# Operands of the first four blocks copied across the partition halves by ScalarE, and a planner that counts on late softmax loads

## The chip, the cores and the metric

The kernel runs on one core of one Trainium2 chip. The metric is the device time of one execution in microseconds (us); the time before is the median of three runs. One further execution was taken with the hardware profiler, and all rows below come from it.

## What is computed

A sequence of 4 x 4096 tokens with 192 channels goes through a dynamic convolution (each of 8 heads weighs the last 7 tokens with a softmax of its own 7 weights), and the result through a gated feed-forward layer with 1536 hidden channels.

```python
w = np.exp(weight_gen - max over the 7 taps)
w = w / (sum over the 7 taps + 1e-09)
out[b, s, h, g] = sum over k of w[b, s, h, k] * x_pad[b, s + k, h, g]
x = out.reshape(B * S, 192)
gate = 1 / (1 + exp(-(x @ w_gate)))
val = x @ w_val
return (gate * val) @ w_out
```

All matrix products are to full 32-bit precision, so each operand is split into a high and a low part, and a product is made of three.

## The kernel before, in words

**Blocks and units.** The 16384 tokens are cut into 32 blocks of 512 (`N`), the 1536 hidden channels into 12 slices of 128 (`NF`). A unit is one slice of one block; there are 384, numbered from 0 here, and block n starts with unit 12n. The unit's work is the same everywhere. TensorE multiplies the block's operands with the slice's weights (`main_jobs`, line 839), ScalarE takes the sigmoid of the gate (line 894), VectorE multiplies it with the value into `h` (line 897), ScalarE rounds that to `hh` (line 900), VectorE takes the rest `hl` (line 903), and two units later (`LAG = 2`) TensorE multiplies `hh` and `hl` with the output weights, in the same stream of instructions as that unit's own products. "Product u" below means line 897 of unit u. TensorE works in two halves of 64 rows that run side by side, so each operand must be there in both halves of the partitions.

**Operands of a block.** `attention(n)` makes them. VectorE multiplies the tokens with the softmax weights and adds up seven products (lines 622 and 636), once for 128 channels x 512 tokens ("head") and once for the 64 remaining channels, folded to 128 x 256 ("tail"). ScalarE rounds the sums to the high parts of `A` and `T` (lines 713 and 754), VectorE makes the low parts (lines 716 and 757). `As` is `A` with its partition halves exchanged, and `T` also needs its other half: for block 0 ScalarE copies them (lines 730 to 736 and 773 to 779: `As` high and low for two halves, `T` high and low for two halves, eight copies); for all later blocks `swap` (line 651) does it with four DMAs. `A`, `As` and `T` have two buffers each.

**Softmax parts.** The taps' weights are loaded in ten parts (`softmax`): part 0 for block 0, part 1 for block 1, part 2 for blocks 2 and 3, and then seven parts of 2048 tokens, four blocks each: part 3 for blocks 4 to 7, part 4 for blocks 8 to 11, and so on. A part is loaded into one of two buffers `w` (line 445), VectorE takes the maximum (456), subtracts (463), ScalarE takes exp (473, which needs another table than the sigmoid and so two table loads), VectorE sums (482), inverts (488, 491) and multiplies (495), and DMAs store the result to DRAM (527), from where `load_wb` reads it back spread over the partitions as `wb` and `wt` (599).

**Weights.** The 12 slices of the weights are loaded and split by `convert` (lines 351 to 412: five instructions on VectorE, four on ScalarE, six matmuls of line 406 to 408); unit f of block 0 needs slice f, so the twelve conversions stand among the first units.

**The order.** Every engine and the DMA queue (SP) works strictly in the order in which the program gives it instructions. That order comes from `Plan`: each piece of work has an engine, a cost in us, what it depends on, which buffers it needs and a due time, and `Plan.order` lets a clock run over these costs and always takes, on each engine, the ready piece that is due first. DMAs are reckoned with `BANDWIDTH`, fixed times at start and end, and a `MARGIN` for those after `EARLY` us (line 200). So a changed cost can move any instruction on any engine.

```python
dma_free = max(dma_free, t + dur + self.DMA_START) + o.nbytes / self.BANDWIDTH
o.end = dma_free + self.DMA_END + (self.MARGIN if t > self.EARLY else 0.0)
```

Of the kernel before, what the change touches and what calls it, by code (L numbers as in the profile page):

```python
# [21 lines left out]
INF = 1e18  # L22
# [14 lines left out]
class Plan:  # L37
# [9 lines left out]
    WINDOW = 0.15  # L47
    BANDWIDTH = 215e3
    DMA_START, DMA_END = 0.6, 1.0
# [11 lines left out]

    def op(self, engs, fn, deps=(), alloc=(), uses=(), due=INF, table=None, nbytes=0, late=0.0, after=(), lag=None, port=True):

        o = Op(
            len(self.ops), engs, fn, [d for d in deps if d is not None], list(alloc),
            [k for _, k in alloc] + list(uses), due, table, nbytes, late,
            [d for d in after if d is not None], lag, port and ("dve" in engs or "pool" in engs),
        )  # L70
        for d in o.deps + o.after:
            d.succ.append(o)
        for k in o.uses:
            self.key_uses.setdefault(k, []).append(o)
        self.ops.append(o)
        return o
# [19 lines left out]
    def order(self):  # L96
# [69 lines left out]
        while todo:  # L166
# [31 lines left out]
            if e == "sp":  # L198
                dma_free = max(dma_free, t + dur + self.DMA_START) + o.nbytes / self.BANDWIDTH
                o.end = dma_free + self.DMA_END + (self.MARGIN if t > self.EARLY else 0.0)  # L200
            else:
                o.end = t + dur
# [14 lines left out]
def conv_gated_ffn(ctx: ExitStack, tc: tile.TileContext, xt, wg, wcat, outT):  # L217
# [88 lines left out]

    LAG = 2
    units = [(n, f) for n in range(NB) for f in range(NF)]
    due = {}
# [36 lines left out]
    def convert(f, due=INF):  # L346
# [63 lines left out]
        def lows(a, z, to, K_):  # L410
# [4 lines left out]

        o_abs = op({"act": act(CT)}, f_abs, [o_ld], alloc=[("ce", E)], uses=[RW])
        o_cl = op({"dve": dve2(CT)}, f_clamp, [o_abs], uses=[E])
# [5 lines left out]
        o_sum = op(  # L423
            {"pe": 1.7}, f_sum, [o_hi, o_rs], alloc=[("ph", KH), ("pt", KT)], uses=[E, C]
        )
# [10 lines left out]
    def softmax(b, t0, T, base, due=INF):  # L436
# [9 lines left out]

        o_ld = op({"sp": SP}, ld, alloc=[("w", key)], nbytes=P * K * L * 4, due=due)
        step = 64 if L % 64 == 0 else L
# [251 lines left out]
    def attention(n):  # L700
# [23 lines left out]
        for rows, to in ((LOW, UP), (UP, LOW)):  # L724
            if n:
                done.append(swap(A, As, slice(0, N), slice(0, N), rows, to, [lo]))
            else:

                def f_shi(buf, e, rows=rows, to=to, ACC=ACC):
                    nc.scalar.copy(buf[As][to, 0, :], buf[ACC][rows, :])  # L730

                def f_slo(buf, e, rows=rows, to=to):
                    nc.scalar.copy(buf[As][to, 1, :], buf[A][rows, 1, :].bitcast(F32))

                done.append(op({"act": act(N)}, f_shi, [last], uses=[As, ACC], after=[hi]))
                done.append(op({"act": act(N)}, f_slo, [lo], uses=[A, As]))

# [12 lines left out]
        for i, rows in enumerate((LOW, UP)):  # L750
# [15 lines left out]
            los.append(op(both(M2), f_tlo, [his[-1]], uses=[T, ACT_]))  # L766
            if n:
                done.append(swap(T, T, own, own, rows, UP if i == 0 else LOW, [los[-1]]))
            else:
                to = UP if i == 0 else LOW  # L770

                def f_shi(buf, e, rows=rows, to=to, own=own):
                    nc.scalar.copy(buf[T][to, 0, own], buf[ACT_][rows, :M2])

                def f_slo(buf, e, rows=rows, to=to, own=own):
                    nc.scalar.copy(buf[T][to, 1, own], buf[T][rows, 1, own].bitcast(F32))

                done.append(op({"act": act(M2)}, f_shi, [lastt], uses=[T, ACT_], after=[his[-1]]))
                done.append(op({"act": act(M2)}, f_slo, [los[-1]], uses=[T]))
        ready[n, 2] = done + his + los  # L780
# [263 lines left out]
```

## Time and profile before

| | before |
|---|---|
| median of 3 runs | 1319.13 us (1317.28 to 1320.64) |
| profiled execution, its own time | 1317.17 us |
| its span, first to last instruction | 1315.4 us |
| TensorE matmuls busy | 1273.6 us, 97% of the span |
| VectorE busy | 1040.1 us, 79% |
| ScalarE busy | 605.8 us, 46% |
| GpSimd busy | 133.8 us, 10% |
| mean granted TensorE clock | 0.982 of full |
| DMA, share of 16 engines' span | 47.2% |

The span is what the profile's rows cover; the execution's own time has 1.77 us around it, and lies 1.96 us under the median of the runs. A matmul's busy time counts overlapping matmuls once and is longer when the clock is lower, so a high busy share does not say that the engine runs at its peak: the number of matmuls in a stretch of fixed length says more.

### The profile page before, as it was taken

How to read it: one execution, taken by the hardware profiler on the slowest of the kernel's cores; microseconds unless marked ns; L12 is line 12 of the kernel's file. 1: busy time of each engine (PE TensorE's matmuls, PEld its weight loads, DVE VectorE, ACT ScalarE, POOL GpSimd, SP SyncE). 2: the span in 40 equal slices, each digit the busy share in tenths (PEclk: the TensorE clock that was granted, in tenths of full speed). 3: DMA queues.
4: the chain of work that ended last, by engine and by line, in shares of the span. 5: the costliest groups of instructions: out<-in, count | busy, mean ns of one | idle time of the engine just before them, and what ended most of it. 6: DMA issues, size and time to landing. Idle time of an engine off the chain costs nothing.

```text
span 1315.4 us, 29736 instructions
## 1 busy us (share of the span) xinstructions
PE 1273.6 (97%) x10860; PEld 1071.0 (81%) x10860; DVE 1040.1 (79%) x1904; ACT 605.8 (46%) x1016; POOL 133.8 (10%) x1477
## 2 busy tenths in 40 slices
PE   5989999899999999999999999999999999999998
PEld 3667888678788888888888888888888888888886
DVE  9898989799988887777788777778887777886443
ACT  4744544354544444444444444444444444444443
POOL 0000111001011111111111111111111111111110
PEclk7989999989899999999999999999999999999999
DMA  4578498846545544444554344445534444211100
GB/s 124 164 189 166 115 174 177 211 120 165 139 113 133 133 97 104 115 116 109 126 133 114 93 117 113 117 114 133 123 97 110 111 118 109 69 37 38 37 13 14
DMA packets 57826, 151.30 MB, mean 115 GB/s; under 512 B 10832, under 2 KB 29136, under 8 KB 57680
## 3 DMA queue, kind: packets, MB, share of 16 engines
q1 hardware_dynamic: 57680, 149.40, 47.2%
q8 instruction: 86, 1.41, 0.5%
q14 instruction: 60, 0.49, 0.1%
HBM read 108.86 MB, written 16.14 MB: 95 GB/s over the span
## 4 chain that ended last, share of the span: by engine, by line
PE 78%; DVE 14%; DMA 3%; issue 2%; ACT 2%; SPq 0%; POOL 0%; DVEq 0%; POOLq 0%; ACTq 0%
PE bank L839 77%; DVE acc L636 2%; DVE h L897 2%; DVE hl L903 2%; DVE prod L622 2%; DMA w<-in_weight_gen 2%; DMA wt<-ws 1%; DVE m L482 1%; DMA wb<-ws 1%; DVE m L456 1%; PE bank L406 0%; DVE prod L675 0%; DVE acc L695 0%; DVE acc L622 0%; DVE m L491 0%
## 5 line engine op out<-in xcount | busy, mean ns | idle before, releaser
L839 PE MATMUL bank<-hh,W 64*128 64x512 f32 x2304 | 773.4, 389 | 1.4 <-POOL seen L837 0.7
L839 PE MATMUL bank<-As,W 64*128 64x512 f32 x2304 | 653.5, 390 | 0.0
L839 PE MATMUL bank<-T,W 64*128 64x512 f32 x2304 | 648.1, 389 | 0.0
L839 PE MATMUL bank<-hl,W 64*128 64x512 f32 x1536 | 596.8, 389 | 6.2 <-DVE hl L903 5.9
L839 PE MATMUL bank<-A,W 64*128 64x512 f32 x2304 | 479.1, 390 | 11.5 <-DVE h L897 9.8
L900 ACT CAST hh<-h 128x512 fp32r<-128x512 f32 x384 | 238.6, 622 | 537.0 <-DVE h L897 535.7
L839 PEld LDWEIGHTS bank<-hh,W 64*128 64x128 f32 x2304 | 425.9, 185 | 41.7 <-POOL seen L837 2.5
L839 PEld LDWEIGHTS bank<-T,W 64*128 64x128 f32 x2304 | 426.6, 186 | 38.5
L839 PEld LDWEIGHTS bank<-As,W 64*128 64x128 f32 x2304 | 425.6, 186 | 38.7
L897 DVE TENSOR_TENSOR h<-bank,sg 128x512 f32<-128x512 f32 x384 | 262.6, 684 | 162.8 <-PE bank L839 161.5
L839 PEld LDWEIGHTS bank<-A,W 64*128 64x128 f32 x2304 | 291.8, 186 | 52.4 <-DVE h L897 11.2
L903 DVE TENSOR_TENSOR hl<-h,hh 128x512 fp32r<-128x512 f32 x384 | 263.0, 685 | 87.2 <-ACT hh L900 83.4
L839 PEld LDWEIGHTS bank<-hl,W 64*128 64x128 f32 x1536 | 284.2, 185 | 35.7 <-DVE hl L903 10.5
L894 ACT ACTIVATE sg<-bank 128x512 f32<-128x512 f32 x384 | 230.4, 601 | 119.7 <-PE bank L839 115.7
L837 POOL MEMSET seen<- 1x1 f32 x1471 | 133.0, 90 | 1175.6 <-PE bank L839 1175.2
L636 DVE TENSOR_TENSOR acc<-acc,prod 128x512 f32<-128x512 f32 (+1 forms) x372 | 202.0, 547 | 0.9
L622 DVE TENSOR_TENSOR prod<-x,wb 128x512 f32<-128x512 f32 x186 | 121.7, 678 | 0.1
L622 DVE TENSOR_TENSOR prod<-xt,wt 128x256 f32<-128x256 f32 x186 | 76.9, 414 | 0.0
L757 DVE TENSOR_TENSOR T<-acc,T 64x256 fp32r<-64x256 f32 x64 | 26.6, 416 | 1.0
L754 ACT CAST T<-acc 64x256 fp32r<-64x256 f32 x64 | 25.8, 403 | 2.5 <-DVE acc L695 1.7
L946 ACT COPY ev<-bank 64x512 f32<-64x512 f32 x32 | 18.8, 586 | 16.2 <-PE bank L839 16.1
L406 PE MATMUL bank<-ce,eye 128*128 128x512 f32 (+1 forms) x48 | 19.9, 501 | 5.0 <-DVE prod L675 3.6
(54 smaller groups left out, 346.2 us busy)
## 6 DMA issues: line engine op xcount, KB each, us to landing
wb<-ws SPq DMA_DIRECT2D x62, 896.0 KB
wt<-ws SPq DMA_DIRECT2D x62, 448.0 KB
As<-A SPq DMA_DIRECT2D x62, 256.0 KB
x<-in_x SPq DMA_DIRECT2D x32, 259.0 KB
out<-osb SPq DMA_DIRECT2D x32, 256.0 KB
T<-T SPq DMA_DIRECT2D x62, 128.0 KB
raw<-in_w SPq DMA_DIRECT2D x12, 576.0 KB
xt<-in_x SPq DMA_DIRECT2D x64, 65.5 KB
```

Of the source, the lines that this page charges most:

```text
L406: nc.tensor.matmul(dst, eye[:, 0].bitcast(F32), buf[E].bitcast(F32)[:, a:z], start=True, stop=False)
L622: nc.vector.tensor_tensor(out=buf[prod(k)][:, :cols].rearrange("p (i t) -> p i t", t=M2), in0=buf[X][:, k : k + cols].rearrange("p (i t) - ...
L636: ENG[e].tensor_tensor(out=a, in0=a, in1=buf[prod(k)][:, :cols], op=ALU.add)
L754: nc.scalar.copy(buf[T][rows, 0, own], buf[ACT_][rows, :M2])
L757: ENG[e].tensor_tensor(out=buf[T][rows, 1, own], in0=buf[ACT_][rows, :M2], in1=buf[T][rows, 0, own].bitcast(F32), op=ALU.subtract,)
L837: turn = nc.gpsimd.memset(seen, 0.0)
L839: ins = nc.tensor.matmul(buf[dst], w, m, start=start, stop=stop)
L894: nc.scalar.activation(out=buf[k["sg"]], in_=buf[k["g"]], func=AF.Sigmoid)
L897: nc.vector.tensor_tensor(out=buf[k["h"]], in0=buf[k["v"]], in1=buf[k["sg"]], op=ALU.mult)
L900: nc.scalar.copy(buf[k["hh"]], buf[k["h"]])
L903: ENG[e].tensor_tensor(out=buf[k["hl"]], in0=buf[k["h"]], in1=buf[k["hh"]].bitcast(F32), op=ALU.subtract)
L946: nc.scalar.copy(buf[EV][LOW, :], buf[PT][UP, :])
```

## The change

Blocks 0 to 3 now get their exchanged halves from ScalarE's copies, and blocks 4 to 31 by DMA. The planner reckons with 190 instead of 215 GB/s, with 12 us more for every softmax load that is issued after its first 60 us, with 0.06 us more for one ScalarE instruction of a conversion and with 1.85 instead of 1.7 us for a conversion's matmuls. Nothing else is different in the source; the order of the instructions is, on every engine.

```diff
-    BANDWIDTH = 215e3
+    BANDWIDTH = 190e3
...
-                o.end = dma_free + self.DMA_END + (self.MARGIN if t > self.EARLY else 0.0)
+                o.end = dma_free + self.DMA_END + (self.MARGIN + o.more if t > self.EARLY else 0.0)
...
     LAG = 2
+    EARLY_BLOCKS = 4
...
-        o_abs = op({"act": act(CT)}, f_abs, [o_ld], alloc=[("ce", E)], uses=[RW])
+        o_abs = op({"act": act(CT) + 0.06}, f_abs, [o_ld], alloc=[("ce", E)], uses=[RW])
...
-            {"pe": 1.7}, f_sum, [o_hi, o_rs], alloc=[("ph", KH), ("pt", KT)], uses=[E, C]
+            {"pe": 1.85}, f_sum, [o_hi, o_rs], alloc=[("ph", KH), ("pt", KT)], uses=[E, C]
...
-        o_ld = op({"sp": SP}, ld, alloc=[("w", key)], nbytes=P * K * L * 4, due=due)
+        o_ld = op({"sp": SP}, ld, alloc=[("w", key)], nbytes=P * K * L * 4, due=due, more=12.0)
...
-            if n:
+            if n >= EARLY_BLOCKS:
                 done.append(swap(A, As, slice(0, N), slice(0, N), rows, to, [lo]))
...
+            to = UP if i == 0 else LOW
+            if n >= EARLY_BLOCKS:
+                done.append(swap(T, T, own, own, rows, to, [los[-1]]))
+                continue
...
+            done.append(op({"act": act(M2)}, f_shi, [lastt], uses=[T, ACT_], after=[his[-1]]))
+            done.append(op({"act": act(M2)}, f_slo, [los[-1]], uses=[T]))
```

**VectorE at units 58 and 59, and the queue of the DMAs.** Part 5 of the softmax lies in `w_68`, part 6 in `w_67`. This is VectorE's order before, from product 57 on (`h_93` is product 57, `h_92` product 58):

```order
L897 TENSOR_TENSOR h_93<-bank,sg_91 128x512
L456 TENSOR_REDUCE m_70<-w_68 128x64
L463 TENSOR_TENSOR w_68<-w_68,m_69 128x7x64
L903 TENSOR_TENSOR hl_97<-h_93,hh_94 128x512
L463 TENSOR_TENSOR w_68<-w_68,m_70 128x7x64
L456 TENSOR_REDUCE m_69<-w_67 128x64
L897 TENSOR_TENSOR h_92<-bank,sg_90 128x512
```

Now part 6 comes at product 78 (`h_92`), with only part 5's last multiplication (line 497, the changed kernel's number for 495) ahead of it:

```order
L899 TENSOR_TENSOR h_92<-bank,sg_90 128x512
L638 TENSOR_TENSOR acc_81<-acc_81,prod_79 128x512
L497 TENSOR_TENSOR w_68<-w_68,m_70 128x7x64
L905 TENSOR_TENSOR hl_97<-h_92,hh_94 128x512
L458 TENSOR_REDUCE m_69<-w_67 128x64
L458 TENSOR_REDUCE m_70<-w_67 128x64
```

The queue's order around the load of part 6 is now this; the load (line 447) stands behind block 10's `x_63` and `wb_72`, whose buffers VectorE gives free with block 8's last head multiplication, and that stands behind product 66:

```order
L329 DMA x_63<-in_x 128x518
L601 DMA wb_72<-ws_132 128x1x1792
L447 DMA w_67<-in_weight_gen 128x896
L657 DMA As_87<-A_85 64x1024 x2
L657 DMA T_89<-T_89 64x2x256 x2
```

So VectorE's first use of part 6 has moved from product 57 to product 78, and its load can be issued 12 products ahead of that; before, the queue issued it between products 55 and 56.

**VectorE from product 26 on.** Before, one softmax part (part 4, in `w_67`) has its maximum and subtraction there, one or two instructions between the unit's own (`h_92` is product 26):

```order
L897 TENSOR_TENSOR h_92<-bank,sg_90 128x512
L456 TENSOR_REDUCE m_70<-w_67 128x64
L463 TENSOR_TENSOR w_67<-w_67,m_69 128x7x64
L903 TENSOR_TENSOR hl_99<-h_92,hh_96 128x512
L463 TENSOR_TENSOR w_67<-w_67,m_70 128x7x64
L897 TENSOR_TENSOR h_93<-bank,sg_91 128x512
```

Now parts 3 (`w_68`) and 4 (`w_67`) come there together:

```order
L899 TENSOR_TENSOR h_92<-bank,sg_90 128x512
L458 TENSOR_REDUCE m_69<-w_68 128x64
L458 TENSOR_REDUCE m_70<-w_68 128x64
L905 TENSOR_TENSOR hl_99<-h_92,hh_96 128x512
L465 TENSOR_TENSOR w_68<-w_68,m_69 128x7x64
L465 TENSOR_TENSOR w_68<-w_68,m_70 128x7x64
L899 TENSOR_TENSOR h_93<-bank,sg_91 128x512
L458 TENSOR_REDUCE m_69<-w_67 128x64
L458 TENSOR_REDUCE m_70<-w_67 128x64
L465 TENSOR_TENSOR w_67<-w_67,m_69 128x7x64
L465 TENSOR_TENSOR w_67<-w_67,m_70 128x7x64
L484 TENSOR_REDUCE m_69<-w_68 128x64
```

Between products 27 (`h_93`) and 28 there are now eight instructions of the softmax (behind the last row shown come product 27's `hl`, one more of line 484 and two short ones of line 490) where five stood; line 484 is the changed kernel's number for 482.

**ScalarE ahead of block 1.** Before, the last conversion's copy is followed by the rounding of block 1's sums and by the units' own work:

```order
L412 CAST W_125<-bank 128x64
L713 CAST A_85<-acc_83 128x512
L754 CAST T_89<-acc_81 64x256 x2
L900 CAST hh_94<-h_93 128x512
L894 ACTIVATE sg_90<-bank 128x512
```

Now the eight copies stand there, around product 10's rounding (`hh_95`) and ahead of unit 11's sigmoid (`sg_91`), and VectorE makes the low parts of block 1 behind product 10, where it made them behind product 8:

```order
L715 CAST A_85<-acc_83 128x512
L732 CAST As_87<-acc_83 64x512
L756 CAST T_89<-acc_81 64x256 x2
L902 CAST hh_95<-h_92 128x512
L735 CAST As_87<-A_85 64x512
L732 CAST As_87<-acc_83 64x512
L735 CAST As_87<-A_85 64x512
L775 CAST T_89<-acc_81 64x256
L778 CAST T_89<-T_89 64x256
L775 CAST T_89<-acc_81 64x256
L778 CAST T_89<-T_89 64x256
L896 ACTIVATE sg_91<-bank 128x512
```

## Rows read from the trace of the kernel before

**Rows 1.** Windows of 40 us: busy us (count), granted clock, DMA share, GB/s.

```profile
80.00:120.00 40.00, 32.33 (x214) 25.03 (x215) 35.97 (x71) 16.83 (x28) 2.32 (x26) 0.83 0.82 174
...
400.00:440.00 40.00, 40.00 (x356) 34.25 (x354) 31.64 (x60) 18.30 (x32) 4.38 (x49) 1.00 0.48 117
```

**Rows 2.** Timeline of VectorE, steady part: start, us, instruction, idle before and releaser.

```profile
418.14 0.69 DVE L897 TENSOR_TENSOR h<-bank,sg 128x512 f32<-128x512 f32 x1 [0.92 <-PE bank L839]
...
430.84 0.69 DVE L897 TENSOR_TENSOR h<-bank,sg 128x512 f32<-128x512 f32 x1 [1.10 <-PE bank L839]
```

**Rows 3.** Timeline of VectorE, products 57 and 62 and the wait between.

```profile
251.17 0.68 DVE L897 TENSOR_TENSOR h<-bank,sg 128x512 f32<-128x512 f32 x1
...
263.00 0.90 DVE L456 TENSOR_REDUCE m<-w 128x64 f32<-128x448 f32 x1 [8.61 <-DMA w<-in_weight_gen]
...
279.51 0.69 DVE L897 TENSOR_TENSOR h<-bank,sg 128x512 f32<-128x512 f32 x1 [0.20 <-PE bank L839]
```

**Rows 4.** The chain that ended last, at the load of part 6.

```profile
245.90 17.01 DMA w<-in_weight_gen
```

**Rows 5.** Timeline of VectorE, products 7, 8 and 14 and work between.

```profile
70.34 0.69 DVE L897 TENSOR_TENSOR h<-bank,sg 128x512 f32<-128x512 f32 x1 [1.20 <-PE bank L839]
70.95 0.68 DVE L622 TENSOR_TENSOR acc<-x,wb 128x512 f32<-128x512 f32 x1
...
75.77 0.45 DVE L367 TENSOR_SCALAR ce<-ce 128x576 f32<-128x576 f32 x1
...
78.71 1.29 DVE L622 TENSOR_TENSOR prod<-x,wb 128x512 f32<-128x512 f32 x2
...
84.49 0.42 DVE L622 TENSOR_TENSOR prod<-xt,wt 128x256 f32<-128x256 f32 x1
84.83 0.42 DVE L636 TENSOR_TENSOR acc<-acc,prod 128x256 f32<-128x256 f32 x1
...
85.83 0.68 DVE L897 TENSOR_TENSOR h<-bank,sg 128x512 f32<-128x512 f32 x1
...
113.67 0.69 DVE L897 TENSOR_TENSOR h<-bank,sg 128x512 f32<-128x512 f32 x1 [1.24 <-PE bank L839]
```

**Rows 6.** Timeline of TensorE: block 1's first matmuls, behind the unit before.

```profile
98.53 0.84 PE L839 MATMUL bank<-A,W 64*128 64x512 f32 x5
```

**Rows 7.** ScalarE's groups by form: count, busy us, mean ns, idle before.

```profile
L733 ACT CAST As<-A 64x512 fp32r<-64x512 f32 x2 | 1.2, 617 | 0.0
L776 ACT CAST T<-T 64x256 fp32r<-64x256 f32 x2 | 0.8, 403 | 0.0
```

**Rows 8.** Windows after three stalls, TensorE alone: busy us (count), granted clock.

```profile
342.00:348.00 6.00, 5.26 (x24) 0.50 0.28 76
264.00:272.00 8.00, 6.18 (x28) 0.50 0.38 101
...
384.00:386.00 2.00, 1.19 (x5) 1.00 0.00 0
```

**Rows 9.** Timeline of VectorE: products 78 and 82, 90 and 94.

```profile
330.29 0.69 DVE L897 TENSOR_TENSOR h<-bank,sg 128x512 f32<-128x512 f32 x1
...
349.09 0.69 DVE L897 TENSOR_TENSOR h<-bank,sg 128x512 f32<-128x512 f32 x1
...
374.50 0.69 DVE L897 TENSOR_TENSOR h<-bank,sg 128x512 f32<-128x512 f32 x1
...
389.57 0.69 DVE L897 TENSOR_TENSOR h<-bank,sg 128x512 f32<-128x512 f32 x1 [1.05 <-ACT sg L894]
```

**Rows 10.** Timeline of ScalarE, a softmax part's exp behind its table load.

```profile
335.71 1.28 ACT L473 ACT_TABLE_LOAD   x1
337.01 0.95 ACT L473 ACTIVATE w<-w 128x896 f32<-128x896 f32 x1
```

**Rows 11.** Timelines of VectorE: one softmax part alone, products 25 and 30.

```profile
149.31 0.63 DVE L897 TENSOR_TENSOR h<-bank,sg 128x512 f32<-128x512 f32 x1
...
165.16 0.69 DVE L897 TENSOR_TENSOR h<-bank,sg 128x512 f32<-128x512 f32 x1 [0.74 <-PE bank L839]
```

More of the change, by code (lines that the diff above doesn't have):

```diff
@@ L60, in place, with op @@
         self.places[name] = [dict(buf=b, key=None) for b in bufs]
-    def op(self, engs, fn, deps=(), alloc=(), uses=(), due=INF, table=None, nbytes=0, late=0.0, after=(), lag=None, port=True):
+    def op(self, engs, fn, deps=(), alloc=(), uses=(), due=INF, table=None, nbytes=0, late=0.0, after=(), lag=None, port=True, more=0.0):
         o = Op(
@@ L70, in op @@
         )
+        o.more = more
         for d in o.deps + o.after:
@@ L724, in attention, with f_shi, f_slo @@
         for rows, to in ((LOW, UP), (UP, LOW)):
-            if n:
+            if n >= EARLY_BLOCKS:
                 done.append(swap(A, As, slice(0, N), slice(0, N), rows, to, [lo]))
[L727 to L736, printed above, removed]
+                continue
+            def f_shi(buf, e, rows=rows, to=to, ACC=ACC):
+                nc.scalar.copy(buf[As][to, 0, :], buf[ACC][rows, :])
+            def f_slo(buf, e, rows=rows, to=to):
+                nc.scalar.copy(buf[As][to, 1, :], buf[A][rows, 1, :].bitcast(F32))
+            done.append(op({"act": act(N)}, f_shi, [last], uses=[As, ACC], after=[hi]))
+            done.append(op({"act": act(N)}, f_slo, [lo], uses=[A, As]))
         ready[n, 0], ready[n, 1] = [hi, lo], done
@@ L766, in attention, with f_shi, f_slo @@
             los.append(op(both(M2), f_tlo, [his[-1]], uses=[T, ACT_]))
[L767 to L779, printed above, removed]
+            to = UP if i == 0 else LOW
+            if n >= EARLY_BLOCKS:
+                done.append(swap(T, T, own, own, rows, to, [los[-1]]))
+                continue
+            def f_shi(buf, e, rows=rows, to=to, own=own):
+                nc.scalar.copy(buf[T][to, 0, own], buf[ACT_][rows, :M2])
+            def f_slo(buf, e, rows=rows, to=to, own=own):
+                nc.scalar.copy(buf[T][to, 1, own], buf[T][rows, 1, own].bitcast(F32))
+            done.append(op({"act": act(M2)}, f_shi, [lastt], uses=[T, ACT_], after=[his[-1]]))
+            done.append(op({"act": act(M2)}, f_slo, [los[-1]], uses=[T]))
         ready[n, 2] = done + his + los
```

## The prediction

> **What bounds the kernel now.** I read the 40 us windows first, for the number of matmuls in each. Between 400 and 440 us, and much the same in every window from there to the end, TensorE does 356 at the full clock of 2.4 GHz, while VectorE is busy for 31.6 of the 40; in the stretch from 80 to 120 us it does 214, at a mean clock of 0.83 [rows 1]. So the time is TensorE's, and what a change of the order can win lies in the first 400 us. Then I read the timeline of VectorE, whose product of each unit (line 897) makes a clock of the program: in the steady part four units take 430.84 - 418.14 = 12.70 us, 3.175 each [rows 2]. Wherever a number of units takes longer than that, the rest is lost to the end, since TensorE never catches up. Three places are to be seen. From product 57 to 62 the units take 28.34 us where 15.87 would do, around one wait of 8.61 us of VectorE for a softmax load [rows 3]: 12.5 us lost. From product 7 to 14 they take 43.33 instead of 22.2 us, with the last conversions in it [rows 5]. And two bunches of softmax work lose 18.80 - 12.70 = 6.1 us (products 78 to 82) and 15.07 - 12.70 = 2.4 us (90 to 94) [rows 9].
>
> **The softmax load of part 6.** It took 17.01 us from issue to landing, the transfers ahead of it included [rows 4], and VectorE's order wanted it 8.5 us after its issue (245.90, and 263.00 - 8.61 = 254.39) [rows 3, 4]. In VectorE's new order the first use stands 12 products, 38 us, behind the point where the load can be issued, so twice the 17.01 would still be in time. The late softmax of parts 5 and 6 now stands alone, each part spread over four or five products with one or two instructions between a unit's own. Before, part 4 stood so, and products 25 to 30 took 15.85 us, no more than five units [rows 11]. So the whole loss goes: -12.5 us. At worst (0) the wait stays somewhere; more than 12.5 can't be had there.
>
> **Block 1's operands.** Durations are taken as distances between starts: 0.61 us for a 512-column instruction (70.34 to 70.95), 0.34 for a 256-column one, 2.94 for the five of a conversion [rows 5]. Summed so, VectorE's 15.7 us of work between products 7 and 8 of before agree with the 15.49 measured, so the sum of what stands between two products tells when the second comes, wherever it exceeds TensorE's 3.175. In the new order there stand between products 7 and 8: product, two multiplications, two conversions and `hl`, 8.3 us; between 8 and 9 4.7 us; between 9 and 10 8.0 us. Nine conversions precede product 7 in both orders, so I leave it at 70.3 and get product 10 at 91.3. Then block 1's low parts are made, and ScalarE copies: after product 10 (0.7) come its `hh`, about as long as a copy, three copies of 0.617 and four of 0.403 [rows 7], 4.1 us, so TensorE can start block 1 at about 96.3 with some 0.2 for starts. Before, it started at 98.53, directly behind the unit ahead of it [rows 6]: TensorE did not wait for the exchange by DMA, and taking these DMAs away gives nothing by itself (0; bounds 0 and -0.5 for lighter queues). The gain comes after: the new order has 2.4 to 3.6 us, 3.1 in the mean, between each two products from 11 to 25, so product 14 comes at about 106.2 instead of 113.67, -7.5 us. Against it, TensorE has idled for about 4 us before block 1, and after such stalls the rows show the lower clock, 0.50 (1.2 GHz): 5.26 busy us after the one near 341, 6.18 after the one near 257 [rows 8], half of which is lost, 2.6 to 3.1. I take 3.0, so -4.5; the ends are -7.5 (the clock stays) and 0 (the weights `wb` of block 1, now wanted one unit earlier, or of block 2 arrive late as well).
>
> **The new bunch.** Parts 3 and 4 of the softmax now stand together behind products 26 to 29. The sums are 4.0, 6.0, 4.9 and 1.9 us, 16.8 for four units that need 12.7: 4.1 lost. The nearest rows are the two bunches of before: 18.9 us of work took 18.80 from product 78 to 82, so there the sum was the whole price; 12.2 us of work, less than the 12.70, took 15.07 from 90 to 94, so there ScalarE's table loads and exp cost 2.4 [rows 9]. Here both are present and partly lie beside each other: +5.5; ends +3.5 and +7.5.
>
> **The same bunches, later.** The work that stood between products 78 and 82 now stands, instruction for instruction, between 90 and 94, and that of 90 to 94 between 102 and 106. Their 6.1 and 2.4 us stay: 0, between -1 and +1.
>
> **The rest.** ScalarE's eight copies for block 2 and for block 3 are 4 x 0.617 + 4 x 0.403 = 4.1 us a block, spread among several units' sigmoid and rounding on an engine that is busy for 18.3 of 40 us [rows 1]; both blocks are ready units ahead of use, so only the delay of some `hh` by a copy or two counts: +0.5, between 0 and 1.5. The order of the conversions before product 7 is different and its sum to product 1 the same: 0, plus or minus 1. From unit 108 on the orders are alike.
>
> **Sum.** -12.5 - 4.5 + 5.5 + 0.5 = -11.0 us. The profiled execution would take 1317.17 - 11.0 = 1306.2; the median of the runs lies 1.96 above it, so 1319.13 - 11.0 = **1308.1 us**.
>
> **A rule weighed.** ScalarE's row shows 1.28 us for a table load and the exp's start 1.30 us after the load's [rows 10], which is all that I charge for a switch.
> The Trainium skill, on its page "ScalarE: Activation LUTs", section "What ACT_TABLE_LOAD costs", adds a drain of about 1.38 us to the load's 1.28. It also says, under "Rules for kernel authors", to do all functions of one table set before switching, which speaks against two parts whose exps alternate with the sigmoid. The trace bears out the load and shows no drain.
>
> **Rivals.**
> - The clock doesn't fall and nothing but VectorE's sums counts: -12.5 - 7.5 + 4.1 = -15.9, **1303.2**. For it: a stall near 385 us, of 0.8 in a window of 2 us, left the clock at 1.00 [rows 8]; against it: block 1's stall is longer than that.
> - ScalarE's copies ahead of block 1 and the bunch each cost their upper end: -12.5 + 0 + 7.5 + 0.5 = -4.5, **1314.6**. For it: sigmoid and rounding of unit 11 stand behind the copies, so the units after block 1's start may drag.
> - The change doesn't do what it says: a softmax load is late at another place and the 12.5 us are lost there, **1320.6**. Against it: part 6 has 38 us, and the loads of parts 7 and 8 keep the 8 products they had.
> - Slower: block 4's weights. Part 4's first store now stands in SP's queue ahead of block 4's `wb` loads and waits for multiplications that end behind product 30; VectorE wants `wb` behind product 35, about 13.4 us after the loads can be issued. VectorE's wait of 8.61 us cost 12.5 [rows 3], 1.45 per us; so the time passes 1323 only when they land more than 23.5 us after issue, and at 24 it is 1308.1 + 1.45 x 10.6 = **1323.5**. Against it: the slowest landing that I read is 17.01 [rows 4], which would cost 5 us.
> - Every switch of tables costs ScalarE as much again in the bunch as its load shows, 1.28 us [rows 10]: four switches for two parts, +5.1, **1313.2**. Against it: the exp starts right behind the load. The Trainium skill's drain, on the page and in the section named above, would be such a cost.
>
> **How the numbers follow.** The forecast, with a spread of about 4 us from its own bounds, has 0.56; the rivals in their order 0.17, 0.13, 0.05, 0.05 and 0.04. The range takes in the first two rivals and the last, and leaves out the two slow ones and the edges: **1303 to 1315 us**. A measurement of this kernel tells about 0.3%, 4 us, from no change, so "faster" begins below 1315.2: the forecast, the first rival, most of the second and the last give 0.86. Without a difference are parts of the second, third and fourth, 0.09; slower the rest, 0.05.
>
> **What would show it.** In the changed kernel's profile VectorE's wait for `w` of 8.6 us should be gone, and TensorE should have 350 or more matmuls in every 40 us between 230 and 330 us. Product 10 should stand near 91, block 1's first matmul near 96 behind an idle stretch of TensorE with a lower clock after it, product 14 between 106 and 110. Four units from product 26 should take about 18 us. I am wrong if TensorE stalls behind product 35, if a wait for `w` of several us appears, or if units 14 to 26 run slower than 3.2 us each.

## The result, and the profile after

The changed kernel takes 1306.71 us in the median of four runs (1304.95 to 1307.71), against 1319.03 us (1317.28 to 1320.64) for the kernel before beside it: 0.9905 of the time, 95% interval 0.9881 to 0.9930. The forecast was 1308.1 us, 1303 to 1315. The profiled execution took 1305.77 us, its span is 1304.0 us; VectorE's busy time (1040.3 us) is what it was, ScalarE's is 10 us longer (615.6).

The windows of the changed kernel that answer to [rows 1], and the one in which VectorE stood before: us, busy us (count) of TensorE, weight loads, VectorE, ScalarE and GpSimd, granted clock, DMA share, GB/s.

```profile
80.00:120.00 40.00, 37.22 (x283) 29.36 (x283) 36.22 (x73) 21.72 (x41) 3.38 (x36) 0.96 0.82 183
230.00:270.00 40.00, 40.00 (x356) 34.25 (x354) 39.94 (x80) 18.10 (x31) 4.32 (x49) 1.00 0.82 176
400.00:440.00 40.00, 38.98 (x322) 32.04 (x320) 33.67 (x64) 19.85 (x32) 3.79 (x43) 0.96 0.45 108
```

Between 80 and 120 us TensorE now does 283 matmuls instead of 214, from 230 to 270 us the full 356. But between 400 and 440 us it does 322 instead of 356. The softmax work of products 90 to 94 of the kernel before (374 to 390 us there) stands in this window now, at products 102 to 106, and costs more: 16.64 us from product 102 to 106, where it took 15.07 [rows 9].

The products in VectorE's timeline of the changed kernel, in the order 14, 25, 35 (they answer to [rows 5, 11]), 57, 62 ([rows 3]), 90, 94, 102 and 106 ([rows 9]):

```profile
107.00 0.69 DVE L899 TENSOR_TENSOR h<-bank,sg 128x512 f32<-128x512 f32 x1
...
142.54 0.68 DVE L899 TENSOR_TENSOR h<-bank,sg 128x512 f32<-128x512 f32 x1
...
178.34 0.69 DVE L899 TENSOR_TENSOR h<-bank,sg 128x512 f32<-128x512 f32 x1 [1.10 <-PE bank L841]
...
248.44 0.69 DVE L899 TENSOR_TENSOR h<-bank,sg 128x512 f32<-128x512 f32 x1
...
264.31 0.68 DVE L899 TENSOR_TENSOR h<-bank,sg 128x512 f32<-128x512 f32 x1
...
353.56 0.69 DVE L899 TENSOR_TENSOR h<-bank,sg 128x512 f32<-128x512 f32 x1
...
372.65 0.69 DVE L899 TENSOR_TENSOR h<-bank,sg 128x512 f32<-128x512 f32 x1 [0.40 <-PE bank L841]
...
398.75 0.69 DVE L899 TENSOR_TENSOR h<-bank,sg 128x512 f32<-128x512 f32 x1
...
415.39 0.69 DVE L899 TENSOR_TENSOR h<-bank,sg 128x512 f32<-128x512 f32 x1 [2.62 <-issue]
```

From such rows the table below is worked out for every kernel that was run: the us lost by product u, which is its start less the start of product 0, less 3.174 (a unit's time in the steady part) for each unit. Product 0 starts at 33.99 us in the kernel before and at 35.35 in the changed one.

| lost by product | 14 | 25 | 35 | 57 | 62 | 67 | 90 | 106 | 383 | median us, ratio to before (95%) |
|---|---|---|---|---|---|---|---|---|---|---|
| before | 35.2 | 36.0 | 36.1 | 36.3 | 48.7 | 48.8 | 54.9 | 57.2 | 57.0 | 1319.03 |
| changed | 27.2 | 27.8 | 31.9 | 32.2 | 32.2 | 32.1 | 32.6 | 43.6 | 43.5 | 1306.71, 0.9905 (0.9881 to 0.9930) |
| e1, first use later | 36.2 | 37.3 | 37.4 | 37.6 | 37.5 | 43.8 | 49.6 | 52.0 | 52.2 | 1311.57, 0.9962 (0.9949 to 0.9975) |
| e2, copies only | 29.7 | 31.3 | 38.0 | 38.5 | 39.0 | 39.3 | 47.0 | 49.4 | 49.5 | 1309.33, 0.9954 (0.9939 to 0.9969) |
| e3, reckoning only | 33.7 | 35.2 | 40.6 | 40.4 | 44.0 | 43.2 | 49.4 | 51.8 | 51.6 | 1313.03, 0.9976 (0.9961 to 0.9991) |
| e4, no reckoning | 27.9 | 28.8 | 29.8 | 30.0 | 30.0 | 30.6 | 38.4 | 44.6 | 44.5 | 1306.80, 0.9930 (0.9915 to 0.9945) |
| e5, changed again | 27.3 | 27.9 | 31.9 | 32.6 | 32.6 | 32.6 | 33.2 | 44.2 | 44.0 | 1302.72, 0.9903 (0.9880 to 0.9926) |
| e6, exchange by DMA | 29.1 | 29.4 | 33.2 | 33.5 | 33.5 | 33.5 | 33.9 | 45.0 | 44.9 | 1306.09, 0.9917 (0.9892 to 0.9942) |
| e7, part 4 apart | 26.9 | 27.5 | 31.5 | 32.9 | 32.9 | 32.9 | 33.3 | 41.0 | 40.8 | 1303.21, 0.9899 (0.9880 to 0.9918) |
| e8, parts apart | 26.5 | 27.1 | 30.5 | 31.3 | 31.6 | 32.0 | 32.6 | 36.3 | 41.1 | 1304.05, 0.9908 (0.9889 to 0.9927) |
| e9, load earlier | 35.0 | 36.2 | 36.3 | 36.4 | 39.0 | 38.9 | 45.2 | 47.5 | 47.4 | 1307.81, 0.9931 (0.9918 to 0.9943) |
| e10, late parts spread | 27.9 | 28.5 | 32.5 | 32.8 | 32.8 | 32.7 | 33.3 | 33.1 | 33.0 | 1295.03, 0.9833 (0.9820 to 0.9847) |
| e11, spread, no reckoning | 27.9 | 28.8 | 29.7 | 29.9 | 29.9 | 30.6 | 34.6 | 34.4 | 34.3 | 1296.08, 0.9844 (0.9831 to 0.9858) |
| e12, part 4 spread too | 26.5 | 27.0 | 29.2 | 29.2 | 29.4 | 29.8 | 30.4 | 30.2 | 30.1 | 1293.03, 0.9829 (0.9815 to 0.9844) |

The runs of e1 to e12 were on other chips, on which the kernel before took 1315.6 to 1316.7 us in the median, so kernels of different chips are compared by the ratio. Each row of losses is from one execution; that of e5 took 1306.49 us, the longest of its four (the others 1302.47 to 1302.95), so its row is some 4 us above its median. In the two first rows one reads where the 12.2 us between the last products (1306.67 and 1294.45) come from: 12.5 at products 57 to 62 and 8.0 up to product 14 are won; 4.0 are lost again between 25 and 35, 2.9 net between 62 and 106 (the bunches), and 1.4 because product 0 starts later.

### The profile page after: what moved, and what is told of

Same layout as the page of the kernel before. It is cut to its first block, busy times and chain, and to the rows that moved or that the text cites. A ratio compares the mean times of both kernels' runs of the same rounds, so it can differ in the third digit from the quotient of the medians.

```text
span 1304.0 us, 29730 instructions
## 1 busy us (share of the span) xinstructions
PE 1269.9 (97%) x10860; PEld 1068.8 (82%) x10860; DVE 1040.3 (80%) x1904; ACT 615.6 (47%) x1040; POOL 131.2 (10%) x1477
## 4 chain that ended last, share of the span: by engine, by line
PE 78%; DVE 17%; issue 2%; ACT 2%; DMA 1%; POOL 0%; DVEq 0%; SPq 0%; POOLq 0%; ACTq 0%
PE bank L841 76%; DVE acc L638 3%; DVE h L899 3%; DVE hl L905 3%; DVE prod L624 3%; DMA x<-in_x 1%; PE bank L408 1%; DVE m L458 1%; DVE acc L624 0%; DVE prod L677 0%; DVE acc L697 0%; DVE m L484 0%; DVE w L465 0%; DVE osb L951 0%; DVE cr L394 0%
## 5 line engine op out<-in xcount | busy, mean ns | idle before, releaser
L841 PEld LDWEIGHTS bank<-hh,W 64*128 64x128 f32 x2304 | 425.0, 185 | 43.2 <-issue 3.6
L841 PEld LDWEIGHTS bank<-T,W 64*128 64x128 f32 x2304 | 425.4, 185 | 41.1 <-ACT T L775 2.5
L841 PEld LDWEIGHTS bank<-hl,W 64*128 64x128 f32 x1536 | 283.9, 185 | 29.8 <-DVE hl L905 4.6
```

The source lines that it names most:

```text
L841: ins = nc.tensor.matmul(buf[dst], w, m, start=start, stop=stop)
```

## The experiments

### What removed the wait for part 6's load: e1, e9, e2, e3, e4

Theory A says that the gain comes from the distance between this load and its first use; its rivals are the copies (B) and the planner's reckoning (C). e1 leaves the load of the kernel before where it is and moves the first use; the sums of part 5 had to move too, as they need the same buffers:

```diff
+        later = {("w", 6): (('f_max', 'f_sub', 'f_exp'), 14.0), ("w", 5): (('f_sum', 'f_eps', 'f_rec'), 15.0)}
...
+                if k in later and o.fn.__name__ in later[k][0]:
+                    t += later[k][1]
```

> The kernel before, with three of the softmax's steps moved in the order and nothing else: the maxima, subtractions and exp of part 6 stand five products later (62 instead of 57), and the sums and inverses of part 5 stand behind them. The load of part 6 stays where it was in the queue. Theory A (the gain comes from the distance between the load of part 6 and its first use): VectorE's wait of 8.61 us is gone and its 12.5 us with it; the moved work lies on units that have none to spare, 1.8 us by VectorE's sums; 1319.0 - 12.5 + 1.8 = 1308.3 us. Theory B (the gain comes from taking the exchange of blocks 1 to 3 off the DMA queues, so that loads land sooner): those DMAs are all still there, the load stays late and the time at 1319, to within 2 us. Theory C (only a planner that reckons with late loads everywhere helps, since a wait taken away here comes back at the next load): 1319 as well, with a wait for w at parts 7 to 9.

The wait is gone here as well (36 to 38 us lost all the way to product 62), but the moved work costs 6.3 us between products 62 and 67, where 1.8 were expected, so the gain is smaller than theory A said. In e1's trace these five units take 22.2 us. VectorE works for all of it but one wait of 1.86 us for a sigmoid, so its work alone is 20.3 us, 4.5 more than five units need: the sum of 1.8 was too low, and the wait stood in no sum.

e9 makes the same test without moved work. In the kernel before it moves one load in the DMA queue and no instruction of another engine:

```diff
+        load5 = next(o for o in order if o.fn.__name__ == "ld" and ("w", 5) in o.uses)
+        def at(o):
+            if o.fn.__name__ == "ld" and ("w", 6) in o.uses:
+                return load5.start + 0.001
+            return o.start
-        for o in plan.run():
+        for o in sorted(order, key=lambda o: (at(o), o.seq)):
```

> The kernel before with one thing moved: the load of part 6 stands directly behind that of part 5 in the DMA queue, twelve rows earlier, some ten products ahead of its first use at product 57 instead of two. No instruction of another engine is moved. Theory A: the wait of 8.61 us goes and nothing takes its place, so the whole 12.5 us are gained by this alone, 1319.1 - 12.5 = 1306.6 us in the terms of the first measurement, 0.990 to 0.991 of the kernel before, as the whole change; by product 62 some 36 us are lost instead of 48.7. The rival that the queue's bandwidth is what was short there: the 0.46 MB only push the loads behind them, VectorE waits for wb or wt of block 8 or 9 instead, and less than half of it is gained.

VectorE's timeline of e9, product 57 and what stands behind it:

```profile
251.48 0.68 DVE L897 TENSOR_TENSOR h<-bank,sg 128x512 f32<-128x512 f32 x1
...
254.63 0.95 DVE L456 TENSOR_REDUCE m<-w 128x64 f32<-128x448 f32 x1
255.51 0.67 DVE L897 TENSOR_TENSOR h<-bank,sg 128x512 f32<-128x512 f32 x1
256.11 0.95 DVE L456 TENSOR_REDUCE m<-w 128x64 f32<-128x448 f32 x1
...
269.89 0.68 DVE L897 TENSOR_TENSOR h<-bank,sg 128x512 f32<-128x512 f32 x1
```

The maximum of part 6 (254.63) follows at once; in the kernel before it waited 8.61 us [rows 3]. Products 57 to 62 take 18.41 us, 2.5 more than five units (15.87), where they took 28.34. So moving the load won 9.9 us there, nothing took its place, and the time is 0.9931 of before (1307.81 against 1316.17 us in the median, 8.4 us less). The whole 12.5 us were expected. The 2.5 us that stay are lost where parts 5 and 6 stand together, and the wait had covered them.

e2, e3 and e4 are single parts of the change. Against the kernel before, e2 has the copies of blocks 1 to 3 alone, e3 the extra time for softmax loads alone; against the changed kernel, e4 leaves out that extra time:

```diff
+    EARLY_BLOCKS = 4
...
-            if n:
+            if n >= EARLY_BLOCKS:
```

```diff
-        o_ld = op({"sp": SP}, ld, alloc=[("w", key)], nbytes=P * K * L * 4, due=due)
+        o_ld = op({"sp": SP}, ld, alloc=[("w", key)], nbytes=P * K * L * 4, due=due, more=12.0)
```

```diff
-        o_ld = op({"sp": SP}, ld, alloc=[("w", key)], nbytes=P * K * L * 4, due=due, more=12.0)
+        o_ld = op({"sp": SP}, ld, alloc=[("w", key)], nbytes=P * K * L * 4, due=due, more=0.0)
```

> The kernel before with the copies of ScalarE for blocks 1 to 3 and nothing else of the change: 215 GB/s, no extra time for softmax loads, the old costs of a conversion. The planner then gives a new order by itself: the load of part 6 can be issued some 16 products ahead of its first use, at product 66. Theory A: no wait for w; VectorE's sums beyond TensorE's 3.174 us a unit come to 39.0 us against 36.1 in the kernel before (two softmax parts together at products 26 to 28, 66 to 68 and 78 to 81); 1319.0 - 12.5 + 2.9 = 1309.4 us. Theory B: as fast as the changed kernel or faster, 1307 or less, whatever the sums. Theory C (the 12 us of extra time are what removes the wait): the wait is still there, 1319 or more.

> The kernel before with the 12 us of extra time for softmax loads and nothing else of the change: the exchange of blocks 1 to 3 is by DMA. In its order part 6 can be loaded some 10 products ahead of its first use, at product 58, where parts 5 and 6 now stand together; so do parts 3 and 4 at products 24 to 27 and parts 7 and 8 at 78 to 81. Theory A: no wait for w, but VectorE's sums are 42.2 us against 36.1; 1319.0 - 12.5 + 6.1 = 1312.6 us. Theory B: no gain, 1319 or more. Theory C: this is the edit that counts, 1307 us, as the changed kernel.

> The changed kernel without the 12 us of extra time for softmax loads, everything else as in it. Part 6 can be loaded some 9 products ahead of its first use at product 78, by the order alone. Theory A: no wait for w of several us; parts 6 and 7 now stand together at products 78 to 81 and parts 8 and 9 at 90 to 93, VectorE's sums are 37.1 us against 31.7; 1306.7 + 5.4 = 1312.1 us. Theory B: the copies are all there, so 1306.7 us, at most 1 more. Theory C: the wait of part 6 comes back, 1319 us.

None of the three has a wait for `w` between products 7 and 78, and none loses more than 3.6 us between products 57 and 62. So theory C falls: the wait is gone without the 12 us that the planner adds (e2, e4) as well as with them alone (e3). Each of these edits moves the plan, and in each of the three orders the load of part 6 can be issued some 9 to 16 products ahead of its use, where it was two in the kernel before. Theory B falls too, as e9 and e3 gain with all the exchange DMAs in place. The times that theory A gave for the three missed all the same: e2 and e3 are some 3 us slower than its sums (0.9954 and 0.9976, where these gave 0.9927 and 0.9952), and e4 is 2 us faster (0.9930 for 0.9948), between what A and B said. What differs among them is the bunches. e2 loses 6.7 us between 25 and 35, e3 5.4, and e4 only 1.0, but 7.8 between 67 and 90. e4 stands at 0.9930, and the intervals of e4 and the changed kernel overlap; in the profiles the reckoning is worth 1.0 us (44.5 against 43.5 lost).

### The way of the exchange: e5, e6

e5 is the changed kernel unaltered. e6 keeps its order and makes the exchange of blocks 1 to 3 by DMA, at the place of the copies and ahead of the loads that the planner had put among them:

```diff
+                if n == 0:
+                    nc.scalar.copy(buf[As][to, 1, :], buf[A][rows, 1, :].bitcast(F32))
+                else:
+                    nc.sync.dma_start(
+                        out=buf[As].bitcast(F32)[to, :, :], in_=buf[A].bitcast(F32)[rows, :, :]
+                    )
```

(and so for `T`; the copies of the high parts are left out for these blocks).

> The changed kernel once more, unaltered, so that the next three are compared with it on the same chip. It should again take 0.988 to 0.993 of the kernel before, and lose 43 to 45 us against TensorE's 3.174 us a unit between its first product and its last, as in its profile.

> The changed kernel in its own order, but the exchange of blocks 1 to 3 is made by four DMAs a block again, in the place of the copies, ahead of the loads of wt that stood beside them; ScalarE's copies of these blocks are left out. Theory A (what block 1 gained comes from the order of VectorE's work between products 7 and 14; the way of the exchange gives nothing by itself): within 1.5 us of the changed kernel, product 14 as in it, 27 to 29 us lost by then. Theory B (the copies are the gain, since the exchange by DMA waits in the queue behind 1.8 MB of wb): block 1 starts late, as in the kernel before, 35 us lost by product 14 and 7 to 8 us more in all. Theory F (the copies are a burden on ScalarE, which the sigmoid of unit 11 waits for): 1 to 3 us less than the changed kernel.

TensorE's waits between 86 and 112 us: engine, line, what it waited for, us in total, times, longest; first e6, then e5.

```profile
PE bank L853 <- DMA As<-A: 3.5, 1, 3.5
```

```profile
PE bank L841 <- ACT As L732: 0.7, 1, 0.7
PE bank L841 <- ACT T L775: 0.7, 1, 0.7
```

With the DMAs TensorE waits 3.5 us for `As`, with the copies 0.7 and 0.7. The DMAs did not stand in a queue: they were issued at 93.92 us, with a DMA share of 0.12 between 92 and 94 us, and TensorE went on at 98.31. By product 14 the difference is 1.8 us, and it is 0.9 at the end. Theory B asked for 7 to 8, theory F for a gain: both fall. Of the 8 us that block 1 gained, some 6 are the order of VectorE's work, 2 the copies. The timed medians (1306.09 and 1302.72, same chip) differ by more than the profiles do, but their intervals overlap.

### The price of softmax parts that stand together: e7, e8, e10, e11, e12

e7 and e8 move parts to given products, with every step behind that unit's `hl`: e7 part 4 alone, e8 the four parts of the lines shown. In e8 the planner was first made to hold parts 7, 8 and 9 until products 150, 180 and 210; when it had made its order, they were moved to the products shown, and the load of part 9 to product 95:

```diff
+        parts = {4: 31, 7: 90, 8: 102, 9: 114}
+        step = dict(f_max=0, f_sub=1, f_exp=2, f_sum=3, f_eps=4, f_rec=4, f_mul=4, st=4)
...
+                u = parts[part] + step[o.fn.__name__]
+                return rounding[u] - 0.001 if o.fn.__name__ == "f_exp" else product[u] + 1.7
```

> The changed kernel with part 4 of the softmax moved from products 27 to 30, where it stands together with part 3, to products 31 to 35, where VectorE has only 1.2 us of a unit's own work; everything else in the changed kernel's order. The theory that two parts together cost what their VectorE work exceeds TensorE's time, and that one part alone in such units costs nothing: the 4.0 us lost between products 25 and 35 of the changed kernel are gone, 4 us less in all. The rival that ScalarE's table switches are the price, two for each part wherever it stands: no difference to 1 us. A second rival, a new wait because block 4's weights now pass part 4's stores in the queue: product 35 not earlier.

> The changed kernel with four parts moved: part 4 to products 31 to 35 as in the run above, and parts 7, 8 and 9, which stand at 90 to 93, 91 to 93 and 102 to 105, to 90 to 94, 102 to 106 and 114 to 118, one part in each block, within the five units in which VectorE has little else to do; no unit has more than 3.6 us of VectorE work there. Theory of VectorE's sums: the 4.0 us of products 25 to 35, the 6.3 of products 90 to 94 and the 4.0 of products 102 to 106 are gone, 14 us less than the changed kernel, some 0.98 of the kernel before. Rival of the table switches: only the part of it that comes from two parts together goes, and each part alone still costs 2.4 us, as part 9 did in the kernel before between products 90 and 94; about 6 us less than the changed kernel.

Both missed: e7 and e8 are no faster than e5. VectorE's timeline of e7 from product 34 to 35 shows why:

```profile
177.91 0.67 DVE L899 TENSOR_TENSOR h<-bank,sg 128x512 f32<-128x512 f32 x1
179.26 0.69 DVE L905 TENSOR_TENSOR hl<-h,hh 128x512 fp32r<-128x512 f32 x1 [0.69 <-ACT hh L902]
179.87 0.29 DVE L490 TENSOR_SCALAR m<-m 128x64 f32<-128x64 f32 x2
180.09 0.96 DVE L493 RECIPROCAL m<-m 128x64 f32<-128x64 f32 x2
180.98 1.09 DVE L497 TENSOR_TENSOR w<-w,m 128x448 f32<-128x448 f32 x2
181.99 0.68 DVE L624 TENSOR_TENSOR acc<-x,wb 128x512 f32<-128x512 f32 x1
182.59 0.68 DVE L899 TENSOR_TENSOR h<-bank,sg 128x512 f32<-128x512 f32 x1
```

The work of this unit is 4.0 us, but product 35 comes 4.68 us after product 34, because VectorE stood 0.69 us waiting for `hh` with all the softmax steps queued behind `hl`. From product 35 to 40 e7 loses another 1.5 us (31.5 to 33.0). That e7's row ends 3.2 us below e5's comes from the later bunches, which e7 did not touch (see the last section). In e8 the three late parts still cost 3.7 us up to product 106 and 2.5 more up to 130, 2.1 a part, against 11.0 for the bunches of e5; and 2.3 us more are lost behind product 130, probably in the order that the planner had made around products 150 to 210 for parts that no longer stood there.

e10 and e11 put half of the steps between the product and `hl`, spread each late part over two blocks, and tell the planner that the moved steps cost nothing:

```diff
+    apart = {7: dict(f_max=(91, 92), f_sub=(93, 93.5), f_exp=(94,), f_sum=(103, 104), f_eps=(105, 105.5), f_rec=(105, 105.5), f_mul=(106, 106.5), st=(106.5,)),
...
+            o.engs, o.table = {e: 0.001 for e in o.engs}, None
...
+            return h[int(u)] + (1.7 if u % 1 else 0.01)
```

(parts 8 and 9 the same, 24 and 48 products later).

> The changed kernel with parts 7, 8 and 9 taken out of products 90 to 105 and spread over two blocks each (maxima, subtractions and exp at products 91 to 94, 115 to 118 and 139 to 142, the rest twelve products later), at most two instructions to a unit, the first of them in VectorE's wait between the product and hl, where the run with the parts apart had them behind hl; the planner is told that these steps cost nothing, so that the order around them is that of an undisturbed block. Theory of VectorE's sums, mended (what counts is the sum with the 0.7 us that VectorE waits for hh): the 11 us between products 90 and 106 are gone but for less than 1 us a part, 8 to 11 us less than the changed kernel, 0.982 to 0.985 of the kernel before. Rival of the table switches: each part still costs 2 us or more, at most 5 us less than the changed kernel, 0.987 or more.

> As the run before this one, but upon the changed kernel without the 12 us for softmax loads, where parts 3 and 4 are not together at product 26 (29.8 us lost by product 35 against 31.9) and part 6 stands alone at 78 once part 7 is taken away. Theory of VectorE's sums: 29.8 us, part 5 2.2 us as there, part 6 as much at the most, and less than 1 us for each of the three spread ones: 34 to 36 us lost in all, against 43.5 to 44.9, 8 to 10 us less than the changed kernel. Rival of the table switches: 38 us or more.

VectorE's timeline of e10, product 92 with a maximum of part 7 in the wait before `hl`, and the windows of TensorE, granted clock, DMA share and GB/s, around parts 7 and 8:

```profile
361.31 0.69 DVE L899 TENSOR_TENSOR h<-bank,sg 128x512 f32<-128x512 f32 x1 [1.00 <-PE bank L841]
361.92 0.96 DVE L458 TENSOR_REDUCE m<-w 128x64 f32<-128x448 f32 x1
362.80 0.68 DVE L905 TENSOR_TENSOR hl<-h,hh 128x512 fp32r<-128x512 f32 x1
364.49 0.69 DVE L899 TENSOR_TENSOR h<-bank,sg 128x512 f32<-128x512 f32 x1 [1.00 <-PE bank L841]
```

```profile
352.00:372.00 20.00, 20.00 (x180) 1.00 0.51 121
392.00:412.00 20.00, 20.00 (x180) 1.00 0.54 130
```

`hl` starts without a wait and VectorE is a full us early for the next product. The three parts cost nothing (33.3 lost by product 90, 33.1 by 106, 33.0 by 383), and e10 takes 0.9833 of the time before where e5 took 0.9903: some 9 us less than the changed kernel. e11 is as good (0.9844): again the reckoning is not what counts. Against e8, e10 has three things different at once (the place before `hl`, two blocks for a part, the planner's costs), and which of them counts was not tested one by one.

ScalarE's timeline of e10 at part 7's exp:

```profile
366.92 1.28 ACT L475 ACT_TABLE_LOAD   x1
368.21 0.95 ACT L475 ACTIVATE w<-w 128x896 f32<-128x896 f32 x1
369.07 0.60 ACT L902 CAST hh<-h 128x512 fp32r<-128x512 f32 x1
369.69 1.28 ACT L896 ACT_TABLE_LOAD   x1
370.98 0.60 ACT L896 ACTIVATE sg<-bank 128x512 f32<-128x512 f32 x1
```

Each load takes 1.28 us and the next activation starts 1.29 us after the load's start. The six switches of these parts cost no time, so the rival falls that a switch has its price wherever it stands. The Trainium skill, on its page "ScalarE: Activation LUTs", section "What ACT_TABLE_LOAD costs", adds a drain of about 1.38 us; these rows show none.

e12 does the same to part 4 besides:

```diff
+    apart = {4: dict(f_max=(30, 30.5), f_sub=(31, 31.5), f_exp=(32,), f_sum=(33, 33.5), f_eps=(34, 34.5), f_rec=(34, 34.5), f_mul=(35, 35.5), st=(35.5,)),
```

> The run with parts 7 to 9 spread, and part 4 besides: its steps stand at products 30 to 35, half of them in VectorE's wait between the product and hl, where the run with part 4 apart had all of them behind hl. Part 3 stays at products 26 to 28, alone. Theory of VectorE's sums with the wait for hh: the 1.5 us that the earlier run lost between products 35 and 40 and the 1.4 us between 30 and 35 are gone, and only the 2 to 3 us of part 3 are left, whose exp stands among the copies for block 3 on ScalarE: 2 to 3 us lost between products 25 and 40 instead of 4.4, 31 to 32 us in all instead of 33.0, 0.982 of the kernel before. Rival (a part between units 30 and 36 delays block 5 whatever its place, since there is no room in VectorE up to product 57): 4 to 5.5 us lost between 25 and 40, as in both runs before.

Between products 25 and 40 it loses 2.2 us (27.0 to 29.2) instead of 4.4 in e10. All of it comes before product 30, where part 3 stands. This is the nearest that the runs come to a test of the place: from product 30 to 40, with part 4 in nearly the same units, e12 loses nothing and e7 2.9 us (30.1 to 33.0); part 4 has six units in e12, though, and five in e7. At 1293.03 us, 0.9829 of the time before, e12 is the fastest of all, though its interval overlaps e10's.

## Why the prediction was right, point by point

- **The softmax load of part 6**, -12.5 us: measured -12.5 (28.34 us between products 57 and 62 became 15.87). The size was right, but it is two things: 9.9 us of waiting (e9) and 2.5 of parts 5 and 6 together, which the new order also took apart. Which edit did it was left open; e2 and e3 show that the copies alone or the extra time alone take the wait away.
- **Block 1's operands**, -4.5 us: measured -6.7 at product 14 (107.00 instead of 113.67), or -8.0 counted from product 0. VectorE's sums held: from product 7 to 10 the units take 8.30, 4.69 and 8.16 us, where the sums gave 8.3, 4.7 and 8.0. The step failed that TensorE "can start block 1 at about 96.3" after a stall of 4 us. These are TensorE's rows in the changed kernel, and two windows behind them (answering to [rows 6, 8]):

```profile
91.82 0.39 PE L841 MATMUL bank<-A,W 64*128 64x512 f32 x1
92.78 1.09 PE L841 MATMUL bank<-A,W 64*128 64x512 f32 x4 [0.57 <-DVE h L899]
...
95.12 0.50 PE L841 MATMUL bank<-As,W 64*128 64x512 f32 x1 [0.71 <-ACT As L732]
...
96.78 0.50 PE L841 MATMUL bank<-T,W 64*128 64x512 f32 x1 [0.65 <-ACT T L775]
```

```profile
98.00:100.00 2.00, 2.00 (x12) 0.50 1.06 165
102.00:104.00 2.00, 2.00 (x22) 1.00 0.66 134
```

It began at 91.82 with `A`, whose high part ScalarE rounds ahead of the copies, and paid three short waits, 1.9 us in all, two of them for copies. The clock fell to 0.50 (1.2 GHz) behind them all the same, and was back at full in the window from 102 us. From its first matmul to product 14 block 1 took 15.2 us, where the forecast had 9.9 (96.3 to 106.2) and 3.0 more for the clock. So the start came 4.5 us earlier than forecast and the way behind it was 2.3 us longer; that the time of product 14 is so near (107.00 for 109.2) is in part luck.
- **The exchange by DMA gives nothing by itself** (0, bounds 0 and -0.5): in the trace of the kernel before TensorE waits for no DMA between 86 and 112 us, as was read; no run put the copies into that order. In the new one, where block 1's low parts stand two products later, e6 shows that the copies are worth 0.9 to 1.8 us. The bounds were drawn from the wrong order.
- **The new bunch** of parts 3 and 4, +5.5 us (3.5 to 7.5): measured 4.1 between products 25 and 35. The four units from product 26 took 16.72 us, where VectorE's sum was 16.8, so the sum alone, 4.1, was the better term; the 1.4 added for tables and exp was not paid.
- **The same bunches, later**, 0 within 1: measured +2.9 (8.5 us lost between products 62 and 106 before, 11.4 in the changed kernel), outside the bounds. The work did not grow; 1.6 of it lies in the last bunch (16.64 us for 15.07), where the clock fell. See below.
- **The rest**, +0.5: the copies of blocks 2 and 3 cost nothing that shows. Block 2's stand between 119 and 126 us, and from product 14 to 25 0.6 us are lost (0.8 before, 0.3 in e6 without these copies). Block 3's stand between 142 and 150 us, at the new bunch, and its four units take 16.74 us in e6, as long as with them. The other order of the conversions put three instructions of one ahead of product 0, which comes 1.4 us later; product 1 comes 1.5 later, more than the 1 that was allowed, and product 7 only 0.6.
- **The rivals.** The clock that doesn't fall: its condition failed at block 1, though the gain there came near its 7.5 and the bunch was its 4.1; the later bunches it had wrong. The copies at their upper end: product 11 did wait 2.73 us for its sigmoid behind the copies, but the units from 11 to 14 then came 3.1 to 3.2 us apart. A load late elsewhere, and block 4's weights: from 70 to 420 us none of the computing engines waits for a DMA. The tables: no.
- **The signs.** Product 10 (92.04), product 14 and the 350 or more matmuls came as said, block 1's first matmul did not. One sign of being wrong showed, by a hair: units 14 to 26 take 3.25 us each, over the 3.2; they took 3.28 before, so it was drawn too narrow.

Against the forecast, block 1 was better by 3.5 us, the bunch by 1.4 and the rest by 0.5, the later bunches worse by 2.9 and the start by 1.4. These errors nearly cancel, so the sum of -11.0 missed the measured -12.3 by only 1.3, less than block 1's term or the later bunches' were off: that is luck. The largest term, the wait for part 6, was right in mechanism and size.

## What to carry to other kernels

When a strict order is planned, look first at each load's distance from its issue to its first use in the trace, and move the load in the queue: one row moved here was worth 8.4 us and touched nothing else. Then look for optional work that bunches: put it where the engine that feeds the bottleneck has room, into the waits that are there anyway (here between a product and the instruction that waits for its rounding), one or two instructions at a time (e10 did both at once). Sums of busy time don't show whether it fits; the waits between dependent instructions belong to them. And a changed cost in a planner changes everything behind it, so test its parts in a frozen order.

## What was not expected of the hardware

VectorE's same instructions in the same order cost 3.9 us between products 102 and 106 in e5 and 2.4 in e7, which runs 1.8 us ahead there. These are product 106 and windows of all engines, with the columns of the windows above: first e5, then e7.

```profile
416.12 0.69 DVE L899 TENSOR_TENSOR h<-bank,sg 128x512 f32<-128x512 f32 x1 [2.61 <-issue]
...
404.00:412.00 8.00, 6.97 (x54) 5.39 (x50) 6.27 (x13) 6.47 (x8) 0.62 (x7) 1.00 0.27 60
412.00:416.00 4.00, 4.00 (x22) 3.17 (x24) 1.51 (x3) 0.60 (x1) 0.33 (x4) 0.57 0.25 61
```

```profile
412.79 0.69 DVE L899 TENSOR_TENSOR h<-bank,sg 128x512 f32<-128x512 f32 x1 [1.07 <-ACT sg L896]
...
404.00:412.00 8.00, 6.97 (x52) 4.81 (x50) 6.32 (x12) 5.55 (x8) 0.54 (x6) 1.00 0.09 19
412.00:416.00 4.00, 4.00 (x39) 3.72 (x38) 1.40 (x3) 2.02 (x5) 0.53 (x6) 1.00 0.44 119
```

TensorE had been idle for 1.03 us of the eight before in both; then it ran at 0.57 of its clock in e5 and at full in e7, and VectorE's wait was 2.61 us in one and 1.07 in the other. The clock fell there in the changed kernel (0.64 from 412 to 416 us) and in e6 too; in the kernel before it stayed at full behind the same work (1.00 from 388 to 392 us, after 1.03 us of idle from 380 to 388). So the same short stall may or may not be followed by the low clock. By these rows the clock accounts for some 1.5 us of the 2.9 by which the later bunches are dearer than before; no run held the clock alone, and the rest stays open.
